# Ten weight blocks converted at other slots: a change to the slot table of an attention and feed-forward kernel

## The chip, the cores and the metric

The kernel runs on one core of a Trainium2 chip. The metric is the time on the device in microseconds (us), as the median of several runs. TensorE (PE) does matmuls and transposes, VectorE (DVE), ScalarE (ACT) and GpSimd (POOL) work elementwise, and SyncE (SP) issues the transfers between the chip's main memory and its on-chip memory. PSUM is the memory of eight banks into which TensorE writes.

## The reference

The input is four batches of eight heads, 576 positions and 64 features a head. Attention is a causal softmax mixed with a memory read-out by a gate of each head; its output, 2304 tokens of 512 features, goes through a feed-forward network of 512 to 2048 to 512 with a sigmoid gate.

```python
scores = where(causal, -1e9, q @ k.T / sqrt(D));  a = softmax(scores);  local = a @ v
q_p = phi(q);  mem_out = (q_p @ M_prev) / (q_p @ z_prev + 1e-6)
x = g * mem_out + (1 - g) * local          # g = sigmoid(beta) of each head
h = x @ w_in
out = (h * sigmoid(1.702 * h)) @ w_out     # w_in, w_out come as 64-bit floats
```

## The kernel before

**Attention.** Two heads make a pair, a batch has four pairs, and pairs 0 to 15 are worked through one after the other. For a pair, SyncE loads keys and queries into `kqr`; ScalarE copies them to `hi` in the matmul's number format (L378), GpSimd subtracts to get the rest, `lok` and `loq`, and SyncE copies these on the chip into the stacked operands `W`. TensorE multiplies scores into PSUM tiles `ps`: the tail scores from `hi`, `lok` and `loq` in two halves (`s_tail`, L553), the others from `W`. VectorE takes the row maxima (L499), ScalarE the exponentials `a` and `at` (L505), VectorE the sums, GpSimd scales (L508), TensorE transposes into `pt`, ScalarE and VectorE copy out to `e`, and TensorE multiplies with the values into `po`. The result `xf` is stored to `xd`. `hi` and `kqr` have one buffer each, so pair p+1's copy waits until pair p's tail scores have been read from it. In the first batch the first 256 positions are done ahead by another routine; its pairs do the remaining 320.

**First layer.** Its weight is cut into 16 blocks of 128 output columns, its input into chunks of positions: the first batch's 256 and then its 320, later 288 each. A block of a chunk is twelve matmuls into a PSUM tile `pm`, which ScalarE or VectorE copies to `hk` and SyncE stores to `gd`. A chunk needs its whole batch's attention; a block needs its weights converted.

**Conversion of a block (`conv_in`, L757).** The weights come as 64-bit numbers. SyncE loads them to `wraw` (two buffers), ScalarE scales the high words into `ws`, VectorE makes three passes over the bits (L179, L180, L182) to the 32-bit `wr`, ScalarE rounds it to `wi` and GpSimd subtracts to get the low part of `wi`. `ws` is in PSUM and has one bank, in the pool `ps_x`. Blocks 0 to 5 are converted ahead of the pairs. Blocks 6 to 15 are converted at the slots that the table `CONV` (L44) gives.

**Slots.** The program is written out in slots from -7 on. The pairs of the first batch begin at slots 0, 7, 14 and 21, pair 4 at 29, the next ones eight later each. A slot emits its attention steps and conversions in order of priority, and then matmuls of the first layer as filler up to a set amount of TensorE time. The framework then orders each engine's instructions by estimated durations and by their slots. On the chip each engine works in that fixed order and waits where data is not there.

**PSUM banks.** `bank` (L76) hands out the attention's tiles from the four banks of `ps_s`. After the last conversion's slot it also uses the conversions' bank, for every fifth tile:

```python
own = state["slot"] > CONV[-1] + 1 and state["bank"] % 5 == 4
return (ps_x if own else ps_s).tile([128, 512], F32, name=name, tag="ps")
```

The table is used at the end of the program's set-up:

```python
for blk in range(W0, NB):
    at(CONV[blk - W0], 58, lambda blk=blk: conv_in(blk))
```

**Second layer.** After the last pair's slots, its weights are converted and its products summed; nothing of it is touched by the change.

Of the kernel before, what the change touches and what calls it, by code (L numbers as in the profile page):

```python
# [34 lines left out]
def tile_attention_memory_moe(ctx, tc, kq, vq, mem, zz, beta, w_in, w_out, out):  # L35
# [5 lines left out]
    PACE = ((20, 2.2), (60, 2.2), (9999, 2.7))  # L41
    LATE = 20
    W0 = 6
    CONV = [-7, -6, -5, -3, -1, 1, 3, 5, 7, 9]  # L44
    PSUM = bass.MemoryType.PSUM

    def pool(stack, name, bufs=1, **kw):
# [28 lines left out]
    def bank(name):  # L76
        state["bank"] += 1
        own = state["slot"] > CONV[-1] + 1 and state["bank"] % 5 == 4
        return (ps_x if own else ps_s).tile([128, 512], F32, name=name, tag="ps")

    def at(slot, prio, fn):
        assert slot > state["slot"], (slot, state["slot"])
        state["seq"] += 1
        events.setdefault(slot, []).append((prio, state["seq"], fn))
# [623 lines left out]
    def first_moe():  # L708
        after = 0
        for n, (b, _, w) in enumerate(chunks):  # L710
            if n not in xplan:
                while b not in xready:
                    yield 1
                xplan[n] = plan_x(n, state["slot"])
                if n >= 2 * MB:
                    xplan[n + 1] = plan_x(n + 1, state["slot"] + 1)
            for blk in range(NB):
                while blk not in wb or n not in xplan or state["slot"] < xplan[n]:
                    yield 1
                after += len(moe_ps) > 1  # L720
                pp, nm = moe_ps[int(after > LATE)]
                ps = pp.tile([128, 512], F32, name=nm)
                wi = wb[blk]
                k = 0
                for c in range(NK):
                    for s, mv in ((0, 0), (1, 0), (0, 1)):
                        mm(ps[:, :w], wi[:, s, 128 * c:128 * c + 128], xq[n][mv][:, c, :w], k == 0, k == 3 * NK - 1)
                        k += 1
                    yield 0
                gate(ps, n, blk)  # L730
                yield 0
# [25 lines left out]
    def conv_in(blk):  # L757
        wb[blk] = w1[blk].tile([128, 2, DM], F32R, name=f"wi{blk}")
        conv_unit(None, wb[blk], w_in[blk], cnv, {"bufs": 2}, lambda: ps_x, {"tag": "ps"}, att, {"tag": f"qpt{blk % 2}", "bufs": 2})
# [14 lines left out]
    for blk in range(W0, NB):  # L774
        at(CONV[blk - W0], 58, lambda blk=blk: conv_in(blk))
    fill["gen"] = first_moe()
# [274 lines left out]
```

## Time and profile before

| what | value |
|---|---|
| median of three runs | 676.65 us (674.99 to 678.63) |
| the profiled execution's own time | 679.05 us |
| its span, from the first to the last instruction | 677.2 us |
| TensorE busy | 619.3 us, 91% |
| VectorE busy | 473.1 us, 70% |
| ScalarE busy | 428.3 us, 63% |
| GpSimd busy | 280.3 us, 41% |
| mean granted TensorE clock | 0.976 |

Busy time is the sum of an engine's instructions, with overlaps counted once. TensorE's matmuls overlap, so a busy TensorE isn't one at its peak; the number of matmuls in a stretch says more. The share of a whole span is a mean over stages with different limits. The trace gives each instruction's start and duration, and behind it in brackets how long its engine had been idle and what it then waited for.

### The profile page before, as it was taken

To read this page: it belongs to the slowest core of one execution; us is meant where nothing else is said; L and a number is where in the kernel's file an instruction comes from. 1 tells how busy PE (TensorE), PEld (TensorE's weight loads), DVE (VectorE), ACT (ScalarE), POOL (GpSimd) and SP (SyncE) were. 2 spreads that over 40 slices of the span, in tenths; PEclk is the share of its full clock that TensorE was granted. 3 is DMA by queue.
4 is the path that set the end of the run, shared out by engine and by line. 5 is a ranking of instruction groups with operands and counts; after the bars stand their busy time and mean duration, and the time that the engine had idled before them with its cause. 6 is when DMAs were issued, how large, how long until landed. Compare 5 with 4: busy or idle time off the path is not lost.

```text
span 677.2 us, 12458 instructions
## 1 busy us (share of the span) xinstructions
PE 619.3 (91%) x4032; PEld 584.9 (86%) x4032; DVE 473.1 (70%) x1108; ACT 428.3 (63%) x977; POOL 280.3 (41%) x311
## 2 busy tenths in 40 slices
PE   4588898889988799999999999799989999999997
PEld 3578686689986689999999998699978999999997
DVE  5987764767758876677748647996369369648954
ACT  5676545777748784677576635746585765675442
POOL 3747545975637692565494303763400000000000
PEclk9999898979999989999989999699999999999999
DMA  7958769788557666766863126683572660563001
GB/s 256 278 159 262 224 196 234 220 211 233 157 157 216 180 199 187 198 172 172 254 174 99 62 71 236 236 281 123 166 249 79 185 203 1 164 185 119 4 21 70
DMA packets 73537, 116.70 MB, mean 172 GB/s; under 512 B 8320, under 2 KB 53376, under 8 KB 73472
## 3 DMA queue, kind: packets, MB, share of 16 engines
q1 hardware_dynamic: 73472, 115.90, 58.1%
q8 instruction: 32, 0.52, 0.3%
q14 instruction: 33, 0.27, 0.1%
HBM read 63.97 MB, written 27.79 MB: 135 GB/s over the span
## 4 chain that ended last, share of the span: by engine, by line
PE 53%; DMA 14%; DVE 13%; ACT 9%; issue 5%; POOL 2%; SPq 2%; DVEq 0%; ACTq 0%; POOLq 0%
PE pm L91 22%; PE acc L913 12%; PE po L91 8%; PE pt L95 6%; DMA g<-gd 5%; PE ps L91 5%; DMA gd<-hk 4%; DVE ol L110 2%; ACT oh L100 2%; ACT g L876 1%; DVE ps L499 1%; DMA xl<-xd 1%; DMA qr<-in_vq_dram 1%; DVE g L110 1%; POOL a L508 1%
## 5 line engine op out<-in xcount | busy, mean ns | idle before, releaser
L91 PE MATMUL pm<-xh,wi 128*128 128x288 f32 (+2 forms) x1024 | 223.3, 307 | 14.4 <-ACT hk L100 9.6
L91 PEld LDWEIGHTS pm<-xh,wi 128*128 128x128 f32 x1024 | 169.4, 194 | 18.6 <-ACT hk L100 11.5
L913 PE MATMUL acc<-oh,wo 128*128 128x384 f32 x672 | 158.5, 337 | 2.6 <-ACT oh L100 2.3
L91 PE MATMUL pm<-xl,wi 128*128 128x288 f32 (+2 forms) x512 | 154.4, 303 | 0.1
L913 PEld LDWEIGHTS acc<-oh,wo 128*128 128x128 f32 x672 | 119.9, 188 | 4.9 <-ACT oh L100 4.8
L110 DVE TENSOR_TENSOR ol<-g,oh 128x768 fp32r<-128x768 f32 x84 | 79.3, 955 | 62.9 <-ACT oh L100 62.7
L913 PE MATMUL acc<-ol,wo 128*128 128x384 f32 x336 | 99.9, 340 | 2.3 <-DVE ol L110 2.2
L91 PEld LDWEIGHTS pm<-xl,wi 128*128 128x128 f32 x512 | 98.8, 194 | 0.7 <-POOL xl L110 0.3
L508 POOL TENSOR_SCALAR a<-a,sm,g 128x512 f32<-128x512 f32 (+3 forms) x112 | 72.4, 660 | 63.5 <-DVE sm L547 37.6
L100 ACT ACTIVATE oh<-g 128x768 fp32r<-128x768 f32 x84 | 70.2, 840 | 42.5 <-PE acc L913 41.5
L499 DVE CUSTOM_DVE_ANT_0 ps<-ps,mask 128x256 f32<-128x256 f32 (+4 forms) x144 | 69.4, 496 | 19.6 <-PE ps L91 15.4
L505 ACT ACTIVATE a<-ps,nm 128x512 f32<-128x512 f32 (+3 forms) x112 | 60.4, 541 | 33.0 <-DVE nm L499 27.9
L91 PE MATMUL po<-e,vs 128*128 128x320 f32 (+3 forms) x416 | 77.6, 311 | 3.6 <-ACT e L100 3.2
L110 DVE TENSOR_TENSOR e<-pt,e 128x320 fp32r<-128x320 f32 (+1 forms) x120 | 56.5, 487 | 30.1 <-ACT e L100 29.5
L100 ACT ACTIVATE e<-pt 128x320 fp32r<-128x320 f32 (+4 forms) x136 | 55.8, 436 | 27.3 <-PE pt L95 15.1
L91 PEld LDWEIGHTS po<-e,vs 128*128 128x128 f32 x416 | 64.7, 194 | 8.8 <-ACT e L100 3.9
L913 PEld LDWEIGHTS acc<-ol,wo 128*128 128x128 f32 x336 | 61.4, 188 | 5.7 <-DVE ol L110 5.6
L91 PE MATMUL ps<-W 128*128 128x512 f32 (+3 forms) x224 | 59.3, 352 | 4.2 <-DVE e L110 2.9
L100 ACT ACTIVATE hk<-pm 128x288 f32<-128x288 f32 (+2 forms) x86 | 34.4, 407 | 42.1 <-PE pm L91 35.4
L95 PE MATMUL pt<-ident,a 128*128 128x128 f32 x296 | 57.7, 277 | 0.4 <-ACT a L505 0.4
L876 ACT ACTIVATE g<-g 128x768 f32<-128x768 f32 x48 | 40.3, 844 | 22.1 <-DMA g<-gd 20.9
L95 PE MATMUL pt<-ident,at 128*128 128x128 f32 x160 | 41.9, 285 | 4.9 <-ACT e L100 1.3
(145 smaller groups left out, 1027.8 us busy)
## 6 DMA issues: line engine op xcount, KB each, us to landing
g<-gd SPq DMA_DIRECT2D x48, 384.0 KB, 3.8
gd<-hk SPq DMA_DIRECT2D x96, 144.0 KB, 2.3
wraw<-in_w_in_dram SPq DMA_DIRECT2D x16, 512.0 KB, 4.7
wraw<-in_w_out_dram SPq DMA_DIRECT2D x16, 512.0 KB, 4.8
kqr<-in_kq_dram SPq DMA_DIRECT2D x12, 608.0 KB, 5.1
W<-hi SPq DMA_DIRECT2D x24, 272.0 KB, 3.3
W<-loq SPq DMA_DIRECT2D x48, 128.0 KB, 3.4
W<-lok SPq DMA_DIRECT2D x32, 144.0 KB, 3.3
```

What stands on the lines that cost most here:

```text
L91: nc.tensor.matmul(out, l, r, start=start, stop=stop)
L95: nc.tensor.transpose(out, in_, idn)
L100: nc.scalar.activation(out=dst, in_=src, func=AF.Copy, **kw)
L110: (nc.vector if eng == "V" else nc.gpsimd).tensor_tensor(out=dst, in0=a, in1=b, op=op)
L499: nc.vector.tensor_tensor_reduce(out=ps, in0=ps, in1=mk, op0=ALU.add, op1=ALU.min, scale=-0.125, scalar=1e38 if j == 0 else nm[:, j - 1:j] ...
L505: nc.scalar.activation(out=a, in_=ps, func=AF.Exp, scale=-1.0, bias=nm, accum_out=sm)
L508: (nc.vector if eng == "V" else nc.gpsimd).tensor_scalar(out=a, in0=a, scalar1=r, scalar2=gcol, op0=ALU.mult, op1=ALU.mult)
L876: nc.scalar.activation(out=t, in_=t, func=AF.Gelu_apprx_sigmoid)
L913: nc.tensor.matmul(acc[b, j][:, :QN], W[2 * p + kk][:, WPART[i], sp, 128 * j:128 * j + 128], mv[:, kk], start=first and p + kk == 0 and sp ...
```

## The change

The ten entries of `CONV` are the slots of blocks 6 to 15. Before, they run from -7 to 9, that is within the first pair and a half; now from -7 to 24, through the slots of pairs 0 to 3. `CONV[-1] + 1`, from which `bank` lends out the conversions' bank, goes from 10 to 25 with it.

```diff
     W0 = 6
-    CONV = [-7, -6, -5, -3, -1, 1, 3, 5, 7, 9]
+    CONV = [-7, -5, -2, 1, 4, 8, 12, 16, 20, 24]
     PSUM = bass.MemoryType.PSUM
```

What this does to the order of the engines is seen at three places.

ScalarE around the copy of pair 3's keys and queries (`hi<-kqr 128x960`). The blocks' numbers in `wi` are those of buffers; before, wi_1003 and wi_1098 are blocks 14 and 15:

```order
L100 ACTIVATE ms<-mr,gt 128x128
L100 ACTIVATE qpt_1187<-pt 128x256
L100 ACTIVATE e_1251<-pt 128x320
L100 ACTIVATE wi_1003<-wr 128x512
L172 ACTIVATE ws<-wraw 128x512
L100 ACTIVATE hk<-pm 128x256
L100 ACTIVATE wi_1098<-wr 128x512
L505 ACTIVATE a_1314,sum_151<-ps,nm 128x512
L100 ACTIVATE xf<-po 64x320
L100 ACTIVATE hi<-kqr 128x960
```

Now wi_864 is block 10, wi_952 block 11, and wi_1096 block 12:

```order
L100 ACTIVATE wi_864<-wr 128x512
L172 ACTIVATE ws<-wraw 128x512
L100 ACTIVATE hk<-pm 128x256
L100 ACTIVATE e_1072<-pt 128x256
L100 ACTIVATE qpt_1092<-pt 128x256
L100 ACTIVATE wi_952<-wr 128x512
L172 ACTIVATE ws<-wraw 128x512
L100 ACTIVATE hi<-kqr 128x960
L505 ACTIVATE at,tail_154<-ps,nm 128x288 x2
L100 ACTIVATE ms<-mr,gt 128x128
L505 ACTIVATE a_1199,sum_151<-ps,nm 128x512
L100 ACTIVATE wi_1096<-wr 128x512
```

The copy stood behind the last write of block 15 and stands now behind that of block 11 and the scaling of block 12.

TensorE around the second half of pair 2's tail scores (`ps<-hi`, `ps<-lok,hi`, `ps<-hi,loq`), before. Here wi_1098 is block 15:

```order
L91 MATMUL pm<-xh,wi_1098 128x256
L91 MATMUL po<-e_1165,vs 128x320
L91 MATMUL po<-e_1167,vs 128x192
L91 MATMUL po<-e_1167,vs 128x64
L91 MATMUL ps<-hi 128x288
L91 MATMUL ps<-lok,hi 128x288
L91 MATMUL ps<-hi,loq 128x288
L91 MATMUL ps<-W_1091 128x384 x2
```

And now, with both halves and block 10 (wi_864); the products `po` of pair 0's first head stand just ahead of these rows:

```order
L95 MATMUL pt<-ident,qp 128x128
L91 MATMUL ps<-hi 128x288
L91 MATMUL ps<-lok,hi 128x288
L91 MATMUL ps<-hi,loq 128x288
L91 MATMUL pm<-xh,wi_864 128x256
L91 MATMUL ps<-hi 128x288
L91 MATMUL ps<-lok,hi 128x288
L91 MATMUL ps<-hi,loq 128x288
L91 MATMUL pm<-xh,wi_864 128x256
```

The second half stood behind three whole blocks (12 to 14), a first matmul of block 15 and pair 1's transposes, and follows now on the first half with one matmul between them.

ScalarE around the copy of pair 4 (`hi<-kqr 128x1216`), now; wi_1319 is block 14:

```order
L100 ACTIVATE hk<-pm 128x256
L172 ACTIVATE ws<-wraw 128x512
L100 ACTIVATE ms<-mr,gt 128x128
L100 ACTIVATE xf<-po 64x320
L100 ACTIVATE hi<-kqr 128x1216
L100 ACTIVATE wi_1319<-wr 128x512
L172 ACTIVATE ws<-wraw 128x512
L100 ACTIVATE e_1390<-pt 128x320
```

Before, there was no conversion left at this place; now blocks 14 and 15 stand on both sides of the copy.

## Rows read from the trace of the kernel before

**Rows 1.** The page, engines over the whole span: busy us, share, instructions.

```profile
PE 619.3 (91%) x4032; PEld 584.9 (86%) x4032; DVE 473.1 (70%) x1108; ACT 428.3 (63%) x977; POOL 280.3 (41%) x311
```

**Rows 2.** Busy time by stages: from:to, length, engines (instructions), granted clock, DMA.

```profile
core 0: us, PE busy (x) PEld busy (x) DVE busy (x) ACT busy (x) POOL busy (x), PEclk, DMA share, GB/s
18.00:72.00 54.00, 43.62 (x258) 37.29 (x258) 45.39 (x123) 37.52 (x93) 35.06 (x38) 1.00 0.80 234
72.00:94.00 22.00, 18.92 (x110) 16.44 (x111) 16.33 (x36) 10.73 (x24) 11.54 (x11) 0.92 0.62 197
94.00:145.00 51.00, 44.83 (x249) 36.38 (x247) 29.38 (x107) 34.32 (x93) 36.31 (x37) 0.90 0.86 228
...
300.00:400.00 100.00, 97.59 (x748) 96.57 (x747) 68.11 (x214) 64.29 (x182) 50.76 (x59) 0.98 0.52 149
```

**Rows 3.** Timeline of ScalarE, pairs 1 to 5: start, duration, instruction, [idle before].

```profile
42.23 1.00 ACT L100 ACTIVATE hi<-kqr 128x960 fp32r<-128x960 f32 x1 [0.42 <-PE ps L91]
...
54.21 1.00 ACT L100 ACTIVATE hi<-kqr 128x960 fp32r<-128x960 f32 x1
...
93.65 1.00 ACT L100 ACTIVATE hi<-kqr 128x960 fp32r<-128x960 f32 x1
...
106.89 1.22 ACT L100 ACTIVATE hi<-kqr 128x1216 fp32r<-128x1216 f32 x1 [1.67 <-DMA qr<-in_vq_dram]
...
121.56 1.21 ACT L100 ACTIVATE hi<-kqr 128x1216 fp32r<-128x1216 f32 x1
```

**Rows 4.** Timeline of TensorE: pair 2's tail scores, and the second chunk's start.

```profile
78.59 0.30 PE L91 MATMUL ps<-hi 128*128 128x288 f32 x1
...
92.96 0.38 PE L91 MATMUL ps<-hi 128*128 128x288 f32 x1
...
144.92 0.83 PE L91 MATMUL pm<-xh,wi 128*128 128x320 f32 x4
```

**Rows 5.** Timeline of VectorE, the first and the last of five conversions.

```profile
72.32 0.69 DVE L179 TENSOR_SCALAR ws<-ws 128x512 int32<-128x512 int32 x1
73.04 0.70 DVE L180 SCALAR_TENSOR_TENSOR ws<-wraw,ws 128x512 int32<-128x512 int32 x1
...
88.00 0.70 DVE L179 TENSOR_SCALAR ws<-ws 128x512 int32<-128x512 int32 x1 [1.52 <-ACT ws L172]
...
89.98 0.69 DVE L182 SCALAR_TENSOR_TENSOR wr<-wraw,ws 128x512 int32<-128x512 int32 x1
```

**Rows 6.** Timeline of ScalarE: block 11's write and block 12's scaling.

```profile
74.56 0.63 ACT L100 ACTIVATE wi<-wr 128x512 fp32r<-128x512 f32 x1 [2.30 <-DVE wr L182]
75.24 0.66 ACT L172 ACTIVATE ws<-wraw 128x512 f32<-128x512 f32 x1
```

**Rows 7.** The tile wi, first 150 us: ns min/median/max, first and last start.

```profile
L110 POOL TENSOR_TENSOR wi<-wr,wi x16: 1272/1294/1310, 24.1 to 91.4; 128x512 fp32r<-128x512 f32 x16
```

**Rows 8.** Who waited for whom, first 140 us: us in total, times, longest.

```profile
ACT wi L100 <- DVE wr L182: 16.4, 10, 2.6
...
PE pm L91 <- POOL wi L110: 2.5, 1, 2.5
...
PEld pt L95 <- ACT a L505: 1.9, 3, 0.7
```

**Rows 9.** Timeline of TensorE around block 10.

```profile
74.24 0.43 PE L91 MATMUL pm<-xh,wi 128*128 128x256 f32 x1 [2.53 <-POOL wi L110]
...
74.69 0.63 PE L91 MATMUL pm<-xh,wi 128*128 128x256 f32 x2
...
77.88 0.40 PE L91 MATMUL pm<-xh,wi 128*128 128x256 f32 x2
```

**Rows 10.** Timeline of SyncE's queue: two issues that were held, one that wasn't.

```profile
34.30 6.31 SPq L164 DMA_DIRECT2D wraw<-in_w_in_dram  x2
...
82.76 0.33 SPq L164 DMA_DIRECT2D wraw<-in_w_in_dram  x1
```

**Rows 11.** One line of the program, L829: second-layer scaling, ns and first start.

```profile
L829 ACT ACTIVATE ws<-wraw x16: 605/632/659, 411.4 to 467.0; 128x512 f32<-128x512 f32 x16
```

## Prediction

> **What bounds the kernel now.** I read four views, from coarse to fine. The page first: TensorE has work in 91% of the span [rows 1], so a gain has to come from a place where TensorE is not full. The table by stages shows where that is [rows 2]. Between 300 and 400 us TensorE is busy for 97.59 of 100 us with 748 matmuls, 7.5 per us. Between 72 and 145 us it gets through 110 + 249 = 359 matmuls in 73 us, 4.9 per us, and at the dense rate these would be 48 us of work. So some 25 us of TensorE's time are open there. No other engine is full either: VectorE is busy for 16.33 + 29.38 = 45.7 of the 73 us (63%), against 45.39 of 54 (84%) in the stage just before, 18 to 72 us. What bounds 72 to 145 us is the order in which the engines take their work, since each takes it strictly in order.
>
> The row to follow is ScalarE's copy of a pair's keys and queries into `hi` (L378): it opens the preparation of a pair. From pair 1 on it starts at 42.23, 54.21, 93.65, 106.89 and 121.56 us [rows 3]. The steps are 12.0, 39.4, 13.2 and 14.7 us: one of them is three times as long as the others, and it lies where the weight conversions are packed. `hi` has one buffer, so pair 3's copy must wait for the second half of pair 2's tail scores. TensorE does the first half at 78.59 and the second only at 92.96 us [rows 4], because the order puts blocks 12, 13 and 14 and pair 1's transposes between them. In that time VectorE converts five blocks (11 to 15), the first from 72.32, the last from 88.00 to 90.67 us [rows 5].
>
> The first batch's second x chunk ends this stage: its matmuls start at 144.92 us [rows 4], after pair 3 has been stored. From there on TensorE is close to full.
>
> **The change, part by part.** No instruction of the computation is added or removed. Up to about 70 us every engine's rows are the same, though the table's first entries differ: blocks 6 to 10 come out where they were. What moves is blocks 11 to 15.
>
> *Pair 3 starts earlier.* In ScalarE's new order `hi` of pair 3 follows directly on the write of block 11 and the scaling of block 12. Those two instructions start at 74.56 and 75.24 us now and last 0.63 and 0.66 us [rows 6], so `hi` could start at 75.9 us. TensorE's new order brings the second half of pair 2's tail scores directly after the first, behind pair 0's output products. I allow 1.1 us for these and take 77.0 us. That is 93.65 - 77.0 = 16.65 us earlier. 75.9 would make it 17.8.
>
> *Four conversions move behind it.* Blocks 12 to 15 now land in the steps from pair 2 to pair 5. One conversion is three VectorE passes of 0.70, 0.70 and 0.69 us [rows 5], 2.09 us, two passes of 0.66 and 0.63 us on ScalarE and one of 1.29 us on GpSimd [rows 6, 7]. How much of that pushes the pairs back is not shown by any row of before, so I bound it. Below, it is nothing: the step from pair 1 to pair 2 also had conversions in it and took 12.0 us [rows 3]. Above, it is the pace at which the packed conversions follow each other now, (88.00 - 72.32) / 4 = 3.92 us, four times: 15.7 us. I take the VectorE time of the four, 8.36 us, times 45.7 / 73, the share of time in which VectorE had work between 72 and 145 us: 5.2 us. It lies nearer to the lower end since the stage after 94 us has VectorE busy for only 29.38 of 51 us.
>
> *Blocks 12 to 15's matmuls* move into the steps after pair 3's start, where TensorE has the room counted above; the 48 us of work fit the 61 us that would be left. Cost nothing; without that cover a block is twelve matmuls, 12 / 7.5 = 1.6 us at the dense rate.
>
> *SyncE's queue.* The raw loads of the last two blocks and the stores of the results of blocks 11 to 15 now stand among the loads of pairs 3 to 5. An issue is 0.33 us when nothing holds it [rows 10]; two loads and five stores are 2.3 us of a queue that is not on the way. It would cost if a load had to wait for its buffer: two such issues held the queue for 6.31 us at 34.30 us [rows 10]. In the new order the two loads that could do so stand behind pair 4's key load, so pair 4's `hi` does not wait for them, only its query load does. I take nothing, and keep 6 us for the range. The two second-layer loads that stood at the end of the conversions move back too; their first use is at 411.4 us [rows 11].
>
> *PSUM.* `bank` (L78) lends the conversions' bank to the attention from slot 11 on in before, now from slot 26 on. So pairs 2 and 3 run on four banks instead of five. Pairs 0 and 1 did so, and TensorE's transposes waited 1.9 us in all for a score bank to be read [rows 8]. Between nothing and 1.9 us; I count it inside the 5.2.
>
> **Sum.** 16.65 - 5.2 = 11.5 us (rounded) at the start of the second chunk. After that TensorE is full and the order of the rest nearly unchanged, so what is gained stays. On the profiled execution's own time that is 679.05 - 11.5 = 667.6 us. It lies 2.40 us above the median of the runs, so on the median 676.65 - 11.5 = **665.2 us**. A check from the other side: VectorE's 45.7 us of work at the 84% of the stage before would take 54.4 us instead of 73, so more than 18.6 us can't be gained without a denser VectorE than this kernel has shown.
>
> **The rivals.**
> *A smaller gain, by the clock.* After 2.53 us of idleness TensorE's next block ran with two matmuls in 0.63 us where 0.40 is usual, from 74.24 to 77.88 us [rows 9]: the lower of the two levels, and half of those 3.64 us lost, 1.8 us. The new order sets blocks 13, 14 and 15 singly among a pair's transposes and waits, and could bring a low stretch to each. Three of them are 5.4 us: a gain of 6.1, 670.6 us. Against it: the stage from 72 to 94 us mixed matmuls and transposes too, and its mean granted clock of 0.92 [rows 2] is explained by that one stretch (half of 3.64 us is 8% of 22). The Trainium skill (TensorE: Matmul & The Clock Gate, "A second HAM failure mode: psum-queue depth-cycling") says that small gaps between groups of matmuls make the clock fall and rise again and that throughput suffers; by that rule this rival holds, and the trace agrees for the gap at 71.7 us.
>
> *No change.* The conversions cost their full pace wherever they stand: ScalarE waited ten times, 16.4 us in all, for a conversion's last VectorE pass [rows 8], and those waits move along. Four times 3.92 is 15.7 of the 16.65 us gained: 675.7 us. Against it stands the 12.0 us step.
>
> *Slower.* TensorE takes its rows in order, and each late block now has its first matmul ahead of attention work. If a block is not converted when its row comes up, the next pair's scores and transposes wait behind it, then VectorE's maxima and ScalarE's exponentials. Block 10 shows the price: 2.53 us of waiting for GpSimd and 1.8 us for the low clock after it [rows 9]. Five blocks (11 to 15) at 4.3 us are 21.7 us: 676.65 - 11.5 + 21.7 = 686.8 us. It decides from 11.5 / 5 = 2.3 us per block on. For it: the new order was set by estimated durations, and GpSimd was late for block 10 in the same way. Against it: of all sixteen blocks only that one made TensorE wait for GpSimd [rows 8].
>
> **How the numbers follow.** The forecast, a gain of 6 to 17 us, has 0.55; the clock rival 0.12; no change 0.18; slower 0.11; more than 17 us 0.04. A measurement of this kernel can tell about 0.5%, 3.4 us, from no change. So faster 0.71, same 0.18, slower 0.11. The likeliest case alone spans 660 to 671 us. For 8 in 10 the range must take in most of the no-change case: 660 to 677 us.
>
> **What would show it.** In the changed kernel's trace: `hi` of pair 3 near 77 us and the step from pair 2 to 3 below 25 us; the steps to pairs 4 and 5 at 13 to 17 us; the second chunk's first matmul near 133 us; VectorE above 70% busy between 72 and 133 us; the stage from 300 to 400 us as dense as now. I am wrong if TensorE's rows of blocks 11 to 15 show waits above 2 us for a conversion, if pair 4's `hi` comes no earlier than 104 us, or if the second chunk starts early and the end does not move.

## The result

The changed kernel took 682.52 us (median of 20 runs, 677.25 to 687.43), the kernel before 677.11 us (20 runs, 673.27 to 682.92). The ratio is 1.0072, with a 95% interval of 1.0044 to 1.0101: 0.7% slower, where 1.7% faster was forecast and the range ended at 677 us. The ratio leaves out one slow execution of the changed kernel (687.43 us) and is not the quotient of the two medians.

The page of the changed kernel gives the engines the same work in a longer span, 681.5 for 677.2 us [rows 1]:

```profile
PE 615.7 (90%) x4032; PEld 581.2 (85%) x4032; DVE 469.8 (69%) x1108; ACT 429.4 (63%) x977; POOL 278.5 (41%) x311
```

The copies `hi` that open the preparation of pairs 1 to 7, as the timeline of ScalarE has them:

```profile
43.15 1.00 ACT L100 ACTIVATE hi<-kqr 128x960 fp32r<-128x960 f32 x1 [0.42 <-PE ps L91]
...
55.14 1.01 ACT L100 ACTIVATE hi<-kqr 128x960 fp32r<-128x960 f32 x1
...
76.19 0.99 ACT L100 ACTIVATE hi<-kqr 128x960 fp32r<-128x960 f32 x1
...
95.52 1.22 ACT L100 ACTIVATE hi<-kqr 128x1216 fp32r<-128x1216 f32 x1
...
120.11 1.20 ACT L100 ACTIVATE hi<-kqr 128x1216 fp32r<-128x1216 f32 x1
...
135.80 1.22 ACT L100 ACTIVATE hi<-kqr 128x1216 fp32r<-128x1216 f32 x1 [2.08 <-issue]
...
157.76 1.22 ACT L100 ACTIVATE hi<-kqr 128x1216 fp32r<-128x1216 f32 x1
```

Pair 3's copy moved from 93.65 [rows 3] to 76.19 us, where 77.0 was forecast. Pair 4's is still 11.4 us early (95.52 for 106.89). Pair 5's is 1.45 us early (120.11 for 121.56). So the gain was there, and was nearly gone 25 us later. Pairs 6 and 7 (135.80 and 157.76 us) stood at 135.39 and 154.14 us before: a further 3.2 us go in the step between these two, and the last pair's copy is then 3.8 us late (348.22 us for 344.38). The busy time by stages, with the same columns as [rows 2], shows the same:

```profile
core 0: us, PE busy (x) PEld busy (x) DVE busy (x) ACT busy (x) POOL busy (x), PEclk, DMA share, GB/s
18.00:72.00 54.00, 41.86 (x259) 36.01 (x260) 46.04 (x126) 37.26 (x93) 34.49 (x37) 1.00 0.79 233
72.00:94.00 22.00, 22.00 (x141) 19.05 (x140) 14.22 (x39) 13.16 (x33) 14.41 (x15) 1.00 0.79 239
94.00:145.00 51.00, 38.67 (x211) 31.20 (x210) 29.19 (x96) 32.74 (x83) 34.95 (x35) 0.90 0.78 208
300.00:400.00 100.00, 97.97 (x762) 96.85 (x761) 69.20 (x219) 67.68 (x193) 55.76 (x65) 1.00 0.53 152
```

From 72 to 94 us TensorE starts 141 matmuls for 110 before. From 94 to 145 us it starts 211 for 249, and the sum of the two stages is 352 for 359.

What happens between pair 4's copy and pair 5's stands in the timeline of all engines from 109 us on:

```profile
109.92 1.83 PE L91 MATMUL ps<-W 128*128 128x512 f32 x4 [3.06 <-DMA W<-lok]
...
111.36 0.57 DVE L499 CUSTOM_DVE_ANT_0 ps<-ps,mask 128x384 f32<-128x384 f32 x1 [4.15 <-PE ps L91]
...
112.02 0.58 ACT L505 ACTIVATE a<-ps,nm 128x384 f32<-128x384 f32 x1 [5.35 <-DVE nm L499]
...
113.25 0.63 PE L91 MATMUL pm<-xh,wi 128*128 128x256 f32 x2
...
113.35 0.66 POOL L508 TENSOR_SCALAR a<-a,sm,g 128x384 f32<-128x384 f32 x1 [6.20 <-DVE sm L547]
...
117.69 0.53 PE L91 MATMUL ps<-hi 128*128 128x288 f32 x1
```

The first line merges four matmuls. In TensorE's order they are pair 4's first 512-wide score, then the two 384-wide scores of pair 3's second head, then pair 4's score again. The first of them needs pair 4's stacked keys and waits 3.06 us for their landing; pair 3's two, which need nothing of pair 4, stand behind it (in e18 below they run at 106.50 us). VectorE's maximum of pair 3 then starts after 4.15 us of idleness, ScalarE's exponential after 5.35, GpSimd's scaling after 6.20. Four engines stand, each behind the one before it, and then TensorE does two matmuls in 0.63 us where 0.40 is usual [rows 9], the lower of its two clock levels (granted clock 0.50 from 110 to 115 us). The last line is the first half of pair 4's tail scores. Pair 5's copy at 120.11 us has to wait for both halves, and they stand behind a block's matmuls and the output products of a pair.

### The profile page after: what moved, and what is told of

It is laid out like the page before. It is cut to its first block, busy times and chain, and to the rows that moved or that the text cites. A ratio compares the mean times of both kernels' runs of the same rounds, so it can differ in the third digit from the quotient of the medians.

```text
span 681.5 us, 12456 instructions
## 1 busy us (share of the span) xinstructions
PE 615.7 (90%) x4032; PEld 581.2 (85%) x4032; DVE 469.8 (69%) x1108; ACT 429.4 (63%) x977; POOL 278.5 (41%) x311
## 4 chain that ended last, share of the span: by engine, by line
PE 45%; DMA 19%; DVE 15%; ACT 10%; issue 7%; SPq 3%; POOL 1%; DVEq 0%; ACTq 0%; POOLq 0%
PE pm L91 21%; PE acc L913 8%; PE po L91 7%; DMA g<-gd 5%; PE pt L95 5%; PE ps L91 4%; DMA gd<-hk 4%; DVE ol L110 4%; DVE g L110 3%; DMA xl<-xd 2%; ACT g L876 2%; ACT oh L100 1%; DMA xd<-xf 1%; DMA W<-lok 1%; DVE ps L499 1%
## 5 line engine op out<-in xcount | busy, mean ns | idle before, releaser
L508 POOL TENSOR_SCALAR a<-a,sm,g 128x512 f32<-128x512 f32 (+3 forms) x112 | 69.9, 636 | 73.8 <-DVE sm L547 42.4
L91 PE MATMUL po<-e,vs 128*128 128x320 f32 (+3 forms) x416 | 75.8, 306 | 3.5 <-ACT e L100 3.4
L91 PEld LDWEIGHTS po<-e,vs 128*128 128x128 f32 x416 | 62.8, 191 | 7.3 <-ACT e L100 4.1
L91 PE MATMUL ps<-W 128*128 128x384 f32 (+3 forms) x224 | 60.3, 355 | 7.0 <-DMA W<-lok 3.1
```

The lines of the kernel that those rows point to most:

```text
L91: nc.tensor.matmul(out, l, r, start=start, stop=stop)
L508: (nc.vector if eng == "V" else nc.gpsimd).tensor_scalar(out=a, in0=a, scalar1=r, scalar2=gcol, op0=ALU.mult, op1=ALU.mult)
```

## The experiments

Eighteen kernels ran, six to twelve executions of each. Each time is the median of its own runs; each ratio is against runs of the kernel before on the same chip, whose medians were 676.3 to 678.5 us. In the diffs "bank after n" stands for the number in `own = state["slot"] > n and state["bank"] % 5 == 4`, the slot after which the attention is lent the conversions' PSUM bank. It was 10 before the change and 25 after it.

### First four: the bank rule against the conversions

```diff
e1  CONV as before the change;   bank after 25
e2  CONV as changed;             bank after 10
e3  CONV = [-7, -5, -3, 0, 2, 5, 8, 11, 13, 16]     (bank after 17)
e4  CONV as changed;             bank after 33
```

> The old list of conversions with one thing of the change alone: the fifth score bank comes in after slot 25, as the longer list makes it, and not after slot 10. Theory A (the cost is in the conversions of blocks 13 to 15, with their loads and copies, standing among the pairs 3 and 4): the time is that of the kernel before, 677 us, and pair 5's hi stays near 121.6 and the tail scores of pair 6 near 152. Theory B (the cost is the bank rule, by which the planner orders the rows after pair 3 anew): pair 4's first 512-wide score stands ahead of pair 3's last rows, the second x chunk's copies stand ahead of pair 5's exponentials, the tail scores of pair 6 come near 156, and the time is 680 to 684 us.

> The new list of conversions with the fifth score bank after slot 10, as before the change. Theory A: as slow as the changed kernel, 681 to 684 us, with pair 4's stacked-key wait of some 3 us still there. Theory B: the gain at pair 3's hi (16 to 17 us earlier) is kept at least in part, pair 5's hi is at 108 to 115 us, the tail scores of pair 6 at 145 to 152, and the time is 666 to 675 us.

> Conversions at slots -7, -5, -3, 0, 2, 5, 8, 11, 13, 16: spread over the pairs 0 to 2, the last at the start of pair 3, and the fifth bank after slot 17 by the unchanged rule. Theory A: less than half of the cost remains, since one conversion stands among the pairs 3 and 4 in place of three: 673 to 679 us. Theory B: no cost remains, the order around the second x chunk is that of before: 665 to 673 us, pair 3's hi at 76 to 82 us and the second chunk's matmuls some 8 us earlier than 144.9.

> The changed kernel with the fifth bank after slot 33, that is behind all first-batch tail work: no score of pair 4 can take the fifth bank ahead of pair 3's tail scores. Theory A: no change from the changed kernel, 681 to 684 us. Theory B, if the harm is that hoisted score: the wait of 3 us on pair 4's stacked key goes out of the row that holds pair 3's tail score up, pair 5's hi is 5 us or more earlier than 120.1, and the time falls by 3 to 8 us below the changed kernel's; if the harm is only that four banks are fewer than five: 683 to 688 us.

| run | us | ratio (95%) |
|---|---|---|
| e1 | 684.39 | 1.0130 (1.0086 to 1.0174) |
| e2 | 689.93 | 1.0170 (1.0119 to 1.0221) |
| e3 | 681.82 | 1.0071 (1.0038 to 1.0104) |
| e4 | 683.09 | 1.0084 (1.0048 to 1.0119) |

All four were slower than the kernel before, and neither theory fits all of them: A had put e1 at 677, B had put e2 and e3 at 675 or less. Something that neither had named was in all of them. It showed in e3. This kernel stores the attention's last `xd` at 407.51 us, the kernel before at 411.36, so it was 3.9 us ahead there; yet its second layer's first product starts at 490.3 us, for 487.6 before. Between the two lies the last x chunk's load. SyncE's queue in e3, then ScalarE's copies of that chunk, then TensorE:

```profile
434.36 0.33 SPq L825 DMA_DIRECT2D wraw<-in_w_out_dram  x1
434.79 0.57 SPq L692 DMA_DIRECT2D xl<-xd  x1
```

```profile
440.80 1.44 ACT L100 ACTIVATE xh<-xl 128x288 fp32r<-128x288 f32 x4 [2.45 <-DMA xl<-xd]
```

```profile
442.59 0.85 PE L91 MATMUL pm<-xh,wi 128*128 128x288 f32 x2 [2.98 <-ACT hk L100]
...
466.53 0.53 PE L91 MATMUL pm<-xh,wi 128*128 128x288 f32 x2 [1.58 <-ACT hk L100]
```

A load of second-layer weights (`wraw`) stands directly ahead of the chunk's load. The copies `xh` wait 2.45 us for the chunk, the evictions `hk` stand behind them on ScalarE, and TensorE waits 2.98 us for an eviction. In the kernel before, that `wraw` stands behind the chunk's load, and so does one store `gd` more. Nothing in this place was edited: the framework orders the engines' rows by estimated durations, and a small difference 300 us earlier turned these two over.

### Next four: the same rows at the end

`LATE = 12` in place of 20 gives the first layer six more PSUM banks a little sooner once the attention is over. With it the chunk's load stands ahead of that `wraw` in every list tried, and the end of the program has the same order for all.

```diff
e5  CONV = [-7, -6, -5, -3, -1, 2, 5, 8, 11, 14]    (bank after 15), LATE 20
e6  CONV as before the change,                      LATE 12
e7  CONV as changed (bank after 25),                LATE 12
e8  CONV of e3 (bank after 17),                     LATE 12
```

> Conversions at slots -7, -6, -5, -3, -1, 2, 5, 8, 11, 14. TensorE's last 3496 of 3946 rows, and ScalarE's last 685 of 819, stand in the same order as in the kernel before, so only the stage up to about 135 us is ordered anew. Theory C (spreading the conversions gains a little in that stage; what made the kernels so far slower is that other rows further on changed places: the pair of x chunks 1 and 2, and the last chunk's load at 435 us): some 2 to 4 us of TensorE's work ahead from 160 to 400 us, kept to the end, 672 to 675 us. Theory D (a conversion that stands later costs time by itself): 679 to 682 us, and no lead at 160 us.

> The old list of conversions with LATE 12 for 20: first-layer matmuls take the six late PSUM banks eight units sooner after the attention has ended. It is the yardstick for the next two kernels, which have the same rows in the same order around the last chunk's load. No theory differs on it; within 4 us of the kernel before.

> The changed kernel with LATE 12; TensorE's last 2530 of 3946 rows (from about 245 us) are those of the yardstick. Theory C: what is lost up to 250 us remains, 3 to 5 us above the yardstick, and nothing is added behind 400 us. Theory D: the same, 4 to 6 us above the yardstick.

> The conversions at slots -7, -5, -3, 0, 2, 5, 8, 11, 13, 16 with LATE 12; TensorE's last 3496 of 3946 rows are those of the yardstick, so the last chunk's load stands where it stands there. Theory C: the lead of 3 to 4 us that this list had at 400 us is kept, 2 to 5 us below the yardstick. Theory D: 3 to 6 us above the yardstick, as this list was with LATE 20.

| run | us | ratio (95%) |
|---|---|---|
| e5 | 673.51 | 0.9961 (0.9929 to 0.9994) |
| e6, the yardstick | 675.23 | 0.9975 (0.9946 to 1.0004) |
| e7 | 679.99 | 1.0050 (1.0023 to 1.0077) |
| e8 | 673.23 | 0.9944 (0.9917 to 0.9970) |

Theory D falls: e5 and e8 convert later than the kernel before and are faster. Theory C holds in all four, though only e5 and e8 tell it from D. SyncE and ScalarE in e8, the list of e3:

```profile
433.63 0.57 SPq L692 DMA_DIRECT2D xl<-xd  x1
434.29 0.57 SPq L704 DMA_DIRECT2D gd<-hk  x1
435.21 0.33 SPq L825 DMA_DIRECT2D wraw<-in_w_out_dram  x1
```

```profile
438.31 1.45 ACT L100 ACTIVATE xh<-xl 128x288 fp32r<-128x288 f32 x4 [0.93 <-DMA xl<-xd]
```

From the issue of the chunk's load to `xh` it is 4.7 us here and 6.0 us in e3. LATE 12 is worth 0.25% on the old list and 0.22% on the changed one (1.0072 to 1.0050), whose chunk load has no `wraw` more ahead of it than the kernel before has. On e3's list it is worth 1.27% (1.0071 to 0.9944). So the turned-over rows cost e3 about 1%, some 7 us. This clears the view on the first half of the program, and the changed kernel's loss is there: 0.75% above the yardstick.

### Bank rule and conversions apart, all with LATE 12

```diff
e9   CONV as before the change,  bank after 15
e10  CONV of e5,                 bank after 10
e11  CONV as before the change,  bank after 17
e12  CONV of e5,                 bank after 15
```

> The yardstick (old list, LATE 12) with one number changed: the fifth score bank comes in after slot 15, not after slot 10. No conversion moves. ScalarE's order has pair 3's hi 12 rows earlier for it, and TensorE's last 3496 rows are the yardstick's. Theory E (pair 3's hi came late because of the bank rule, not because of conversions): hi at 76 to 85 us, and 1 to 4 us below the yardstick. Theory F (it came late because the conversions of blocks 11 to 15 stood ahead of it): hi stays above 90 us and the time is the yardstick's, or up to 2 us above, for the missing bank.

> LATE 12, conversions at slots -7, -6, -5, -3, -1, 2, 5, 8, 11, 14, but the fifth score bank after slot 10 as with the old list. TensorE's last 3496 rows are the yardstick's; pair 3's hi stands one or two rows from its old place on ScalarE. Theory E: hi at 88 us or later, and no gain over the yardstick (within 1.5 us). Theory F: hi at 76 to 85 us, and 2 to 4 us below the yardstick.

> The yardstick with the fifth bank after slot 17. No conversion moves, but the planner turns over the order from the second x chunk on, as in the changed kernel: TensorE's last 2530 rows alone are the yardstick's, and the second chunk's copies stand ahead of pair 5's exponentials' evictions. If that turn-over is the whole loss of the changed kernel behind 130 us: 3 to 5 us above the yardstick and within 1.5 us of the changed kernel with LATE 12. If the loss belongs to the late conversions: within 1.5 us of the yardstick.

> The two things that gained together: conversions up to slot 14 with the fifth bank after slot 15, and LATE 12. If both gains add, 0.4 + 0.25% below the kernel before: 671 to 673 us, and 2 to 3 us below the yardstick. If the lead is swallowed at the last chunk's load, 674 to 676 us.

```diff
e13  CONV as before the change,  bank after 25
e14  CONV as changed,            bank after 17
e15  CONV of e3,                 bank after 10
e16  CONV = [-7, -6, -4, -1, 2, 5, 8, 12, 16, 20],  bank after 10
```

> The yardstick (old list, LATE 12) with the fifth bank after slot 25, as the changed list sets it. TensorE's last 3507 of 3946 rows are those of the changed kernel with LATE 12, so the two differ in the stage up to about 135 us alone, by where the conversions stand. If the bank rule is most of the changed kernel's loss: 0.4 to 0.8% above the yardstick, 678 to 681 us, and within 1.5 us of the changed kernel with LATE 12. If the conversions at slots 16, 20 and 24 are most of it: 675 to 677 us.

> The changed list with LATE 12 and the fifth bank after slot 17 instead of 25. TensorE's last 3048 rows are those of the changed kernel with LATE 12. If the missing bank during pairs 3 and 4 costs by itself: 1.5 to 3 us below the changed kernel with LATE 12 (680.0). If the late conversions cost: no nearer to the yardstick than 3 us, 678 to 681 us.

> Conversions at slots -7, -5, -3, 0, 2, 5, 8, 11, 13, 16, fifth bank after slot 10, LATE 12; TensorE's last 3543 rows are the yardstick's. If spreading the conversions gains and the early bank gains 0.3% beside it: 670 to 672 us, as with the list up to slot 14. If the conversion at slot 16 costs already: 673 to 676 us.

> Conversions at slots -7, -6, -4, -1, 2, 5, 8, 12, 16, 20, fifth bank after slot 10, LATE 12; TensorE's last 3255 rows are the yardstick's, the second chunk's copies stand late as in the yardstick. If conversions among the pairs 3 and 4 cost by themselves, even with the early bank and an order that is not turned over further on: 675 to 679 us, with pair 4's tail scores or its stacked keys late. If only the bank rule and the turned-over order cost: 669 to 672 us.

Last, the changed kernel itself with one number of it undone (e17, LATE 20), and one run that takes the inversion of 110 us away while nearly all of the bank rule stays (e18, LATE 12):

```diff
e17 (against the changed kernel)
-        own = state["slot"] > CONV[-1] + 1 and state["bank"] % 5 == 4
+        own = state["slot"] > 17 and state["bank"] % 5 == 4
e18 (against the changed kernel)
-    LATE = 20
+    LATE = 12
-        own = state["slot"] > CONV[-1] + 1 and state["bank"] % 5 == 4
+        own = state["slot"] > 23 and state["bank"] % 5 == 4
```

> The changed kernel with one number of it undone: the fifth bank after slot 17, not 25 (LATE stays 20). With LATE 12 the same list and bank gave 669.7 us. Here the last chunk's load stands behind one w_out load more on SyncE than in the kernel before, as it did with the list up to slot 16, where that order cost some 6 us against the same list with LATE 12. If that holds: 673 to 677 us. If that order is harmless: 669 to 672 us. In either case at least 5 us below the changed kernel, if the loss of the changed kernel is what happens with the missing bank around 110 us.

> The changed list with LATE 12 and the fifth bank after slot 23 instead of 25. Up to about 105 us the rows are those of the changed kernel; then pair 4's first 512-wide scores no longer stand ahead of pair 3's second 384-wide scores, which so no longer wait for the landing of pair 4's stacked keys. If that row order was the loss: 669 to 673 us, as with the bank after slot 17, and pair 3's last score near 106 us instead of 110. If it is the bank that is missing in slots 18 to 23: 677 to 681 us.

The ratios of all kernels with LATE 12, by the list of conversions (its last slot) and the slot after which the bank is lent; half of a 95% interval is about 0.003:

| list, last slot | 10 | 15 | 17 | 23 | 25 |
|---|---|---|---|---|---|
| old, 9 | 0.9975 (e6) | 1.0003 (e9) | 1.0010 (e11) | | 1.0014 (e13) |
| 14 | 0.9919 (e10) | 0.9957 (e12) | | | |
| 16 | 0.9916 (e15) | | 0.9944 (e8) | | |
| 20 | 0.9889 (e16) | | | | |
| changed, 24 | | | 0.9867 (e14) | 0.9969 (e18) | 1.0050 (e7) |

In us: e9 676.51, e10 670.40, e11 676.67, e12 673.42, e13 678.77, e14 669.67, e15 672.90, e16 670.74, e18 675.88. With LATE 20, e17 took 673.60 us, 0.9940 (0.9902 to 0.9978). Against what was expected of them, e13, e16 and e17 came as one of their branches had it. e14 came 10.3 us below e7, where 3 at most were expected. e12, e15 and e18 fell between their branches. e11 came 1.4 us above the yardstick, which by its text puts the loss on the late conversions; e14, with the same conversions as the changed kernel, speaks against that.

Down a column, only the conversions move: every step later is faster or the same. With the bank after 10 the lists end at 0.9975, 0.9919, 0.9916 and 0.9889; with the bank after 17 the changed list is 1.4% below the old one (1.0010 to 0.9867). The one exception is the last column, the changed kernel's own (1.0014 to 1.0050, no more than the intervals allow). Along a row, only the bank is lent later: every step is slower or the same. On the old list that is 0.4% from 10 to 25, no more than the intervals allow. On the changed list it is 1.0% from 17 to 23 and 0.8% more from 23 to 25.

One pair with LATE 20 breaks the rule of the rows. e2 and e17 both have the changed list, and in both the last chunk's load is turned over. e2 has the bank after 10 and took 689.93 us (1.0170); e17 has it after 17 and took 673.60 (0.9940). So the number doesn't act simply as a bank that is missing for longer: what it does goes by the order of rows that comes out.

Theories E and F each got one half. The place of pair 3's `hi` follows the bank rule, as E said: without any conversion moved, e9 has it 8.9 us earlier than the kernel before, while e10, with conversions up to slot 14, has it only 5.3 us earlier. But conversions move it as well: e12, with e9's bank and conversions up to slot 14, has it at 76.77 us. ScalarE in e9 and in e10:

```profile
84.80 1.00 ACT L100 ACTIVATE hi<-kqr 128x960 fp32r<-128x960 f32 x1 [3.40 <-PE ps L91]
```

```profile
88.38 1.00 ACT L100 ACTIVATE hi<-kqr 128x960 fp32r<-128x960 f32 x1
```

But the time follows the conversions, as F said: e9 gains nothing over the yardstick, e10 gains 0.56%. An early `hi` is not a gain by itself.

e17 is the forecast with one term taken out. Its stages, the starts of `hi` of pairs 3 to 5, and the second chunk's first matmuls:

```profile
72.00:94.00 22.00, 22.00 (x142) 19.23 (x141) 14.79 (x41) 12.76 (x33) 15.10 (x16) 1.00 0.83 237
94.00:145.00 51.00, 46.45 (x271) 39.85 (x270) 35.47 (x114) 37.16 (x97) 39.06 (x39) 0.90 0.84 235
300.00:400.00 100.00, 98.26 (x753) 97.34 (x752) 64.78 (x203) 62.46 (x177) 45.76 (x54) 0.98 0.47 138
```

```profile
75.92 0.99 ACT L100 ACTIVATE hi<-kqr 128x960 fp32r<-128x960 f32 x1
...
98.56 1.21 ACT L100 ACTIVATE hi<-kqr 128x1216 fp32r<-128x1216 f32 x1
...
112.11 1.22 ACT L100 ACTIVATE hi<-kqr 128x1216 fp32r<-128x1216 f32 x1 [1.23 <-DMA mr<-in_mem_dram]
```

```profile
133.95 1.12 PE L91 MATMUL pm<-xh,wi 128*128 128x320 f32 x4
```

From 72 to 145 us TensorE starts 142 + 271 = 413 matmuls, for 359 before and 352 in the changed kernel. The second chunk starts at 133.95 us, 11.0 us before its old place [rows 4]; 11.5 was forecast. This profiled execution was e17's fastest (670.24 us). e14 differs from e17 in LATE alone, which acts only once the attention is over, and its profiled execution was its slowest (672.15 us): there the second chunk starts at 135.44 us, 9.5 us early. The whole program gains 0.6% and not the 1.3% of e14. Here the last chunk's load stands behind a `wraw` again, and its copies wait:

```profile
436.48 1.45 ACT L100 ACTIVATE xh<-xl 128x288 fp32r<-128x288 f32 x4 [2.30 <-DMA xl<-xd]
```

What goes with the bank rule is seen in the `W` scores, 512 wide and 384 wide, of pairs 3 and 4. TensorE in e18 (bank after 23), where the inversion is gone, and in e14 (after 17):

```profile
106.50 0.60 PE L91 MATMUL ps<-W 128*128 128x384 f32 x2
113.38 0.72 PE L91 MATMUL ps<-W 128*128 128x512 f32 x2
119.47 1.52 PE L91 MATMUL ps<-W 128*128 128x512 f32 x2
122.08 0.76 PE L91 MATMUL ps<-W 128*128 128x384 f32 x2
124.07 0.60 PE L91 MATMUL ps<-W 128*128 128x384 f32 x2
```

```profile
105.27 1.05 PE L91 MATMUL ps<-W 128*128 128x384 f32 x4
113.64 0.73 PE L91 MATMUL ps<-W 128*128 128x512 f32 x2 [0.69 <-ACT e L100]
114.56 1.07 PE L91 MATMUL ps<-W 128*128 128x384 f32 x4
119.14 0.59 PE L91 MATMUL ps<-W 128*128 128x384 f32 x2
```

In e18 pair 3's last score is at 106.50 us, near e14's 105.3, and no longer at 110. Against e7, pair 5's `hi` is 4.6 us earlier (114.45 us for 119.05) and so is pair 15's (344.29 for 348.86); the ratios differ by 0.8%. But the inversion is not all that differs. Pair 4's tail scores start at 109.19 us in e18 and at 116.61 in e7, near the changed kernel's 117.69:

```profile
109.19 0.54 PE L91 MATMUL ps<-hi 128*128 128x288 f32 x1
```

e4 shows that the inversion alone doesn't set pair 5's start. There pair 3's last score is at 109.18 us and no longer stands behind pair 4's 512-wide ones; a 128-wide score of pair 4 has moved ahead instead, and TensorE waits 1.86 us at it. The tail scores come at 117.67 us and pair 5's `hi` at 120.10, as in the changed kernel. This profiled execution was e4's slowest (690.04 us). How the 0.8% divides between the inversion and the place of the tail scores was not tested.

Pair 4's scores begin at the same time in e18 and e14. In e18 the second 512-wide ones come 6.1 us behind the first and the last score is at 124.07 us; in e14 it is at 119.14. That this makes the other 1.0% is not shown. The second chunk starts 3.2 us later in e18 (138.60 us for 135.44), but pair 5's `hi` (114.45 and 114.83) and pair 15's (344.29 and 343.94) stand alike in the two traces. Pair 4's own slots have the fifth bank in either kernel, so the bank rule acts through the rows of pairs 2 and 3 ahead of it; the way from there to pair 4 is not shown.

## Why the prediction was wrong

**The step that failed** is the term on PSUM: "Between nothing and 1.9 us; I count it inside the 5.2." The 1.9 us were what transposes of pairs 0 and 1 waited on four banks. Lending the bank after slot 25 and not after slot 17 costs the changed kernel 1.3% with LATE 20 (e17, 0.9940, against 1.0072), some 9 us, and 1.8% with LATE 12 (e14 against e7), some 12 us. Without it the moved conversions make the kernel faster by 0.6% (e17) and 1.3% (e14). The term was at most 1.9 us and measured 9 to 12, and it set the sign. I priced it as waits for a bank in the order of before; it came with another order of the rows. That order, and not the length of time with four banks, is what e2 points at too: with the bank as early as before it lost more than the changed kernel.

**Pair 3's earlier start** came as forecast, 76.19 us for 77.0. That it carries the gain was wrong as put: e9 has an early `hi` and no gain.

**The four conversions, 5.2 us.** With the bank after 17 the second chunk started 11.0 us earlier in e17 and 9.5 us in e14, where 16.65 - 5.2 = 11.5 was forecast. So that sum came out nearly, but in part by luck: in e17 pair 4's `hi` is only 8.3 us early, with a step of 22.6 us from pair 3 to 4 where 13 to 17 were expected, and the rest is regained behind it. In the changed kernel the steps from pair 3 to 4 and 4 to 5 were 19.3 and 24.6 us, where 13 to 17 were expected.

**"The order of the rest nearly unchanged, so what is gained stays"** was right on the work and wrong on the order. In e17 pair 7's `hi` is 4.2 us early (149.97 us for 154.14) and pair 15's 7.8 (336.55 for 344.38): in that execution the dense stage gives nothing back. In e14's, with the same rows up to there, they are 0.5 and 0.4 us early (153.60 and 343.94), so one trace doesn't settle how much lead is kept. And whether a lead survived the last chunk's load depended on a few rows. LATE 12 is worth 0.04 to 0.25% where no `wraw` was turned over (e5 to e12, the yardstick, the changed list) and 0.7 to 1.3% where one was (e17 to e14, e1 to e13, e3 to e8). In the changed kernel it was not turned over, so this is no part of its loss; it hid the gain of e3 and half of that of e17.

**SyncE's queue at nothing** was wrong in its reason. No load for a pair held the queue for more than 1.75 us (`zb` at 78.42 us), but the landing of pair 4's stacked keys became what TensorE waited for, since a row that needs them had moved ahead of rows that did not.

**The rivals.** The slower one ended on the right side by the wrong mechanism: the longest wait of a matmul for a late block was 1.1 us (for `wi`, at 98.33 us), below the 2.3 us from which that rival decides. The wait was a score's for a transfer. The clock rival does not explain it: the mean granted clock from 94 to 145 us is 0.90 before, in the changed kernel and in e17 alike. Where a wait does bring the lower level (two matmuls in 0.63 us at 113.25 us), it is a consequence. The Trainium skill (TensorE: Matmul & The Clock Gate, "A second HAM failure mode: psum-queue depth-cycling") says that small gaps between groups of matmuls make the clock fall and rise again. The trace bears this out only in part: it shows the lower level behind one wait of 3.06 us, not behind a row of small gaps. The same page ("The mechanism") says that matmuls run strictly in their order, none overtaking another; the rows at 109.92 us agree, where two scores of pair 3 stood behind one of pair 4 whose keys had not landed.

**Of the signs named** three came: pair 3's `hi`, the step from pair 2 to 3 of 21.1 us, and the stage from 300 to 400 us as dense as before. The second chunk started at 142.22 us, 2.7 us early and not near 133, and the end came later. VectorE was to be above 70% busy from 72 to 133 us; it was at 37.63 / 61 = 62%.

**Open.** Why lending the bank later costs the old list at most 0.4% and the changed list 1.8% (from 17 to 25) is not derived. The bank rule and the order that the planner makes of it were never apart: e18 takes the inversion away with two slots of the bank. Why the changed list with the bank after 10 (e2) is the slowest of all is not known: its end was turned over, but so was that of e17, and it was not run with LATE 12. In the changed kernel, e7, e11, e13, e14 and e17 the rows around the second x chunk are turned over too, and in each of their traces the step from pair 6's `hi` to pair 7's is 21.6 to 24.6 us, for 18.7 before and 18.6 in e9. That is the changed kernel's 3.2 us there. But e11 differs from e9 by this order and takes the same time (676.67 and 676.51 us), and e17 has regained its lead by pair 15 while e14 has not, so what it costs in the end stays open.

## What to carry to other kernels

A constant may have a second reader. `CONV[-1] + 1` decided when the attention got its fifth PSUM bank, and through the order of the rows that cost as much as or more than what the change itself gained; price each reader of a number that is edited, and give the second its own number before judging the first. Where a planner orders the rows, compare the whole order and not only the place of the edit: look for a row that waits for a transfer ahead of rows that are ready, and for a bulk load that has slipped ahead of a load on which an engine waits. When several variants are all slower, first give them the same order where they shouldn't differ.

The best kernel here, e14, changes three numbers: the changed list, the bank after slot 17, and LATE 12. It took 669.67 us, 1.3% below the kernel before (0.9837 to 0.9897).

## What the runs showed that I had not expected

Executions of one kernel differ by more than most of the effects studied. e9 ran from 672.43 to 680.91 us, and its profiled execution was its fastest: by the spans it was 3.4 us ahead of the yardstick (670.6 for 674.0), by the medians 1.3 us behind. e17 and e14 have the same rows until the attention is over, and in their traces pair 15's `hi` is 7.4 us apart (336.55 and 343.94 us). A lead of a few us in one trace is therefore weak evidence. And one load of 512 KB and one store that stood ahead of the last chunk's load on SyncE's queue, at 435 us, went with 0.7 to 1.3%, nearly as much as moving the ten conversions gained (1.4% with the bank after 17).
